# Sliding-window attention and a tanh-shrink MLP: scores of two pairs of heads as one group from batch 3 on

## The chip, the core and the metric

The kernel runs on one core of a Trainium2 chip. A core has TensorE (matmuls), VectorE, ScalarE, GpSimd (POOL in the profile), SyncE, and 16 DMA engines that the queues of SyncE (SP) and GpSimd feed. The metric is device time in microseconds, from the start of the program to its end. Several runs were timed, and one execution was recorded by the profiler; the times of single instructions below are from that one.

## The reference

For 8 batches of 8 heads, with 576 positions and 64 channels a head, each position attends to itself and the 63 before it. The heads of a position are then put side by side (512 channels), and 4608 such tokens go through two layers:

```python
scores = (1 / sqrt(64)) * q @ k.T                 # B=8, H=8, S=576, D=64
mask = (rel >= 0) & (rel < 64)                    # rel = row - column
attn = softmax(where(mask, scores, -1e9))
x = (attn @ v).transpose(0, 2, 1, 3).reshape(4608, 512)
h = x @ w_in                                      # 512 x 2048
out = (h - tanh(h)) @ w_out                       # 2048 x 512, float32 out
```

Inputs and output are float32; the kernel computes its matmuls in bf16.

## The kernel before, in words

**One script sets the order.** Every piece of work is a small step function. `PLAN` (L605) is a long text of words such as `Rp.12.2.4`; `play` (L600) calls the step of that name with these numbers, one after the other. The tile framework runs with a manual schedule, so each engine issues its instructions in the order of the words, and the framework adds the waits that the data need. The letters p, a, v and s at the end of a word name the engine: GpSimd, ScalarE, VectorE, SyncE.

**Attention.** The 8 heads of a batch form 4 pairs; pair `g % 4` of batch `g // 4` has heads `g % 4` and `g % 4 + 4`. The 576 positions are cut in 9 windows of 64 queries, and a window needs 128 keys. Scores are computed with the keys in the 128 rows of the result, so a pair has 9 x 2 products of 128 x 64. There are three forms of it:

- Batch 0 (`BY_HEAD`): one product per head and window, with 64 rows of contraction. A product with `hide` first puts a large negative number where the window ends.
- Batches 1 to 3: `Rp.g.grp.bank` (`scores`, L272) computes three windows at once, with 128 rows of contraction; the q of the two heads stands in `qT` as two blocks with zeros beside them. `Rx` (L310) is the exponential of it. In batch 3 the keys are already in `kw`, put there by DMA transposes.
- Batches 4 to 7: `S.g` (`tile_scores`, L297) has 18 products of 64 x 64 contraction rows and queries, from `kw` and `qw`, which DMA transposes fill. The two heads of a pair lie in the upper and lower half of the rows and write two different PSUM banks, 3 and 4; the ninth window goes to columns 448 to 511 of banks 5 and 7. `Sx.g.0` and `Sx.g.1` are the exponentials (128x1024 and 128x128).

`M.g` (`masking`, L398) multiplies the exponentials by the mask on VectorE. `PP.g` (`pv_pairs`, L418) multiplies two pairs with v, whose tile has a column of ones, into banks 5 to 7 (36 products). `DR` and `DN` (L430, L435) divide by the sums. For batches 0 to 2 `Xp`/`Xc` transpose the result on TensorE and copy it into the chunk tile `xT`; from batch 3 on `Y.b` (`x_dma`, L488) does it with two DMA transposes.

**How q and k come in.** For batches 0 to 2 `lk`/`lq` (`load`, L93) load a pair in rows of 96 partitions; `ck`/`cq` (`cast`) put the heads side by side; `Fp`/`Ep` are six transposes on TensorE (L252), and `Fc`, `Ec`, `Ea`, `Eb` (`put`) copy the result out of PSUM. From batch 3 on `lr.b.i.h` (`load_k`, L157) loads 128 rows of k for half of the heads, cast to bf16 on the way, into a tile laid out pair by pair; `tk.b.i` (`tr_k`, L163) is the DMA transpose on SyncE's queue into `kw`. `qr` and `tq` (L168, L173) do the same for q from batch 4 on. For batch 3, `LQ.3` loads all of q as `lq` does, and it goes on by `cq`, `Ep`, `Ea` and `Eb`. `LV.b.i` loads v, and `Z` copies parts of it to the other half of the partitions.

**The layers.** Tokens are taken in 9 chunks of 512. `H.c.m` (`hp_mm`, L504) is one of 16 tiles of the first layer: four matmuls of 128x512 into bank 0, 1 or 2. `A` is the tanh on ScalarE (L516), `G` the subtraction on VectorE (L522). `W.c.s.part` (`yp_mm`, L537) is a quarter of the second layer for 128 tokens: four matmuls. `O.c.s` copies 128 tokens out of PSUM and sends them to memory on SyncE's queue. `H` of a tile waits until `G` has freed the bank two tiles before.

**Queues.** All loads are issued by GpSimd, in the order of the plan; all transposes and outputs by SyncE, in the order of the plan. A DMA that has to wait for its data holds up all behind it in its queue. `U.n` is n matmuls on a tile of zeros (L219) that keep TensorE busy at the start; `i`, `h`, `n` build the identity, `hide` and the mask on GpSimd, `N` puts the mask into PSUM, and `mt`, `mv`, `mq`, `mk` are memsets on VectorE. `wi` and `wo` load the weights.

Of the kernel before, what the change touches and what calls it, by code (L numbers as in the profile page):

```python
# [7 lines left out]
F32 = mybir.dt.float32  # L8
# [7 lines left out]
def kernel(  # L16
# [41 lines left out]
    mask = ps[:, 6, 480:512].bitcast(BF16)  # L58
# [4 lines left out]
    K_BY_DMA = (3, 4, 5, 6, 7)  # L63
    BY_HEAD = (0,)
    BY_TILE = (4, 5, 6, 7)
    NR, NPT, NROW = 2, 4, 3
    SPLIT = 0
    NKR = 4 if SPLIT else NR
# [5 lines left out]
    PT = [const.tile([128, NJ, 128], BF16, name=f"pt{i}") for i in range(NPT)]  # L74
# [4 lines left out]
    qw = [const.tile([128, NP, S], BF16, name=f"qw{i}") for i in range(2)]  # L79
    rows_all = {n: [const.tile([128, H, E * D], BF16, name=f"{n}all{i}") for i in range(2)] for n in "qk"}  # L80
# [72 lines left out]
    def token_rows(b, n="k"):  # L153
        t = rows_all[n][b % 2].rearrange("p h f -> p (h f)")[:, 0:(NF + 1) * H * D]
        return t.rearrange("p (i r h d) -> p i r h d", r=NP, h=2, d=D)

    def load_k(b, i, h):  # L157

        c = min(128, S - 128 * i)
        nc.gpsimd.dma_start(out=token_rows(b)[0:c, i, :, h, :],  # L160
                            in_=k[b, NP * h:NP * h + NP, 128 * i:128 * i + c].rearrange("r p d -> p r d"))

    def tr_k(b, i):  # L163
        c = min(128, S - 128 * i)
        nc.sync.dma_start(out=kw[b % 2][:, :, 64 + 128 * i:64 + 128 * i + c],
                          in_=token_rows(b)[0:c, i].rearrange("p r h d -> p (r h d)"), transpose=True)

    def load_q(b, i, h):  # L168
        c = min(128, S - 128 * i)
        nc.gpsimd.dma_start(out=token_rows(b, "q")[0:c, i, :, h, :],  # L170
                            in_=q[b, NP * h:NP * h + NP, 128 * i:128 * i + c].rearrange("r p d -> p r d"))

    def tr_q(b, i):  # L173
        c = min(128, S - 128 * i)
        nc.sync.dma_start(out=qw[b % 2][:, :, 128 * i:128 * i + c],
                          in_=token_rows(b, "q")[0:c, i].rearrange("p r h d -> p (r h d)"), transpose=True)
# [32 lines left out]
    def pads_q(i):  # L209
        nc.vector.memset(qT[i], 0.0)  # L210

# [60 lines left out]
    def scores(g, grp, bank):  # L272
        sp, js = group(g, grp, bank)
        first = g not in hidden_by_product
        kt = kT[g % NKR] if g // NP not in K_BY_DMA else kw[g // NP % 2][:, g % NP]
# [18 lines left out]
    def tile_spot(j, h):  # L294
        return ps[:, 3 + h, 64 * j:64 * j + 64] if j < 8 else ps[:, 5 + 2 * h, 448:512]

    def tile_scores(g):  # L297
        b, pr = divmod(g, NP)
        for j in range(NJ):
            for h in range(2):  # L300
                r = slice(64 * h, 64 * h + 64)
                nc.tensor.matmul(tile_spot(j, h), kw[b % 2][r, pr, 64 * j:64 * j + 128],  # L302
                                 qw[b % 2][r, pr, 64 * j:64 * j + 64], start=True, stop=True)
# [10 lines left out]

    halves = {}

    def half_rows(s):
        if not halves:
            t = g_pool.tile([128, M, TOK], BF16, tag="gT", name="early")
            t = t.rearrange("p m t -> p (m t)")  # L320
            n = H * 8 * D
            halves["k", 0], halves["q", 0] = t[0:32, 0:n], t[0:32, n:2 * n]
            n = H * 10 * D
            halves["q", 1], halves["k", 1] = t[32:64, 0:n], t[64:96, 0:n]
        return {n: halves[n, s].rearrange("p (h f) -> p h f", h=H) for n in "qk"}

    def half_span(s):
        return 256 * s, 8 + 2 * s

    def load_half(n, s):  # L330
        t0, e = half_span(s)
        nc.gpsimd.dma_start(out=half_rows(s)[n],
                            in_=(q if n == "q" else k)[0, :, t0:t0 + 32 * e].rearrange("h (p e) d -> p h (e d)", e=e))

    def half_bank(s, bank):
        e = half_span(s)[1]
        return ps[:, bank, :].bitcast(BF16)[:, 0:32 * e].rearrange("c (e p) -> c e p", e=e)

    def half_tr(n, g, s, bank):
        src, tp, r = half_rows(s)[n], half_bank(s, bank), {"k0": 0, "q0": 0, "q1": 32, "k1": 64}[f"{n}{s}"]  # L340
        for e in range(half_span(s)[1]):
            for h in range(2):
                nc.tensor.transpose(tp[64 * h:64 * h + 64, e, :], src[:, g + NP * h, D * e:D * e + D],
                                    ident[r:r + 32, r:r + 32])

    def half_put(n, g, s, bank, eng):
        t0, e = half_span(s)
        to = kT[g][:, 64 + t0:64 + t0 + 32 * e] if n == "k" else qp[g][:, t0:t0 + 32 * e]
        move(eng, to.rearrange("c (p e) -> c p e", e=e), half_bank(s, bank).rearrange("c e p -> c p e"))

    def half_group(s, bank):
        n = 4 + s
# [372 lines left out]
```

## Time and profile before

| | us |
|---|---|
| median of three runs | 313.98 (312.68 to 313.98) |
| span of the profiled execution, first to last instruction | 314.8 |
| TensorE busy | 301.9 |
| VectorE busy | 185.5 |
| ScalarE busy | 159.1 |
| GpSimd busy, issue of its DMAs included | 126.4 |
| H matmuls (L508), 576 of 0.22 us a start | 141.2 busy |
| W matmuls (L551), 530 recorded | 132.0 busy |
| first H step (H.0.0) begins | 25.57 |

In the profile's lists a line like `L302 PE MATMUL ps<-qw,kw ... x288` means: line 302 of the kernel, TensorE, output tile `ps` from `qw` and `kw`, 288 of them. Matmuls are pipelined: the busy time of one (194 ns for a 64-column one) is longer than the distance to the next (about 20), so costs on the path are read from starts. PEclk is the granted clock of TensorE, 1.00 for full speed. A bracket at the end of a line, `[2.31 <-DMA kw<-kall]`, is idle time before the instruction and what ended it. The profiled execution took 0.8 us more than the median of the runs.

### The profile page before, as it was taken

The page shows a single profiled execution, that of the slowest core. Times are in us where ns is not written, and L with a number is a line of the kernel's source. Part 1 is how long each engine was busy: PE and PEld are TensorE (multiplying, and loading weights), DVE is VectorE, ACT ScalarE, POOL GpSimd, SP SyncE. Part 2 cuts the span into 40 slices and gives each one's busy share as a digit, 9 for nine tenths or more (in the row PEclk, how much of TensorE's full clock was granted, in tenths as well). Part 3 has the DMA queues.
Part 4 walks back from the last instruction along what each step waited for, and adds up shares of the span by engine and source line. Part 5 has one row for each costly group of instructions (what it writes and reads, how often), then busy time and mean ns, then how long its engine had stood idle before and what let it go on. Part 6 is the DMA issues. An engine that isn't in the chain of part 4 may idle for free.

```text
span 314.8 us, 6266 instructions
## 1 busy us (share of the span) xinstructions
PE 301.9 (96%) x2480; PEld 159.4 (51%) x2510; DVE 185.5 (59%) x320; ACT 159.1 (51%) x286; POOL 126.4 (40%) x180
## 2 busy tenths in 40 slices
PE   7889899999999969999999999999999999999996
PEld 2565555656655534554455445455444444544443
DVE  3586786499976645784766556767645524533410
ACT  3588963698764524623735364445633433343301
POOL 8991656896992884077800965000000000000000
PEclk9999999999999998999999999999999999999999
DMA  9999999999999999999945999991004010000102
GB/s 158 145 179 204 170 205 185 194 148 115 107 132 138 155 141 141 173 99 158 154 78 116 116 156 155 153 130 50 34 35 108 33 67 35 33 33 35 67 33 101
DMA packets 127789, 36.75 MB, mean 117 GB/s; under 512 B 115600, under 2 KB 122256, under 8 KB 127760
## 3 DMA queue, kind: packets, MB, share of 16 engines
q0 software_dynamic: 88000, 18.07, 73.3%
q1 hardware_dynamic: 39760, 18.29, 29.6%
q8 instruction: 19, 0.31, 0.4%
q14 instruction: 10, 0.08, 0.1%
HBM read 36.70 MB, written 9.44 MB: 147 GB/s over the span
## 4 chain that ended last, share of the span: by engine, by line
PE 82%; DMA 5%; POOL 5%; DVE 3%; issue 2%; ACT 1%; SPq 1%; POOLq 0%; DVEq 0%
PE ps L551 37%; PE ps L508 36%; PE ps L425 3%; DMA wi<-in_moe_w_in_dram 3%; DMA kw<-kall 3%; PE ps L302 2%; PE ps L291 2%; POOL kall L109 1%; DVE gT L522 1%; POOL vw L144 1%; POOL qall L109 1%; PE ps L544 1%; PE ps L252 1%; PE ps L474 1%; DVE qt L91 0%
## 5 line engine op out<-in xcount | busy, mean ns | idle before, releaser
L522 DVE TENSOR_TENSOR gT<-ps,th 128x512 bf16<-128x512 f32 x144 | 97.8, 687 | 78.6 <-ACT th L516 77.4
L508 PE MATMUL ps<-xT,wi 128*128 128x512 bf16 x576 | 141.2, 381 | 0.9 <-DVE gT L522 0.5
L551 PE MATMUL ps<-w_out_sb,gT 128*128 128x512 bf16 x530 | 132.0, 380 | 2.0 <-issue 0.7
L516 ACT ACTIVATE th<-ps 128x512 f32<-128x512 f32 x144 | 84.8, 598 | 96.0 <-PE ps L508 93.6
L508 PEld LDWEIGHTS <-wi 128*128 128x128 bf16 x576 | 63.0, 114 | 55.2 <-issue 1.6
L551 PEld LDWEIGHTS <-gT 128*128 128x128 bf16 x560 | 53.5, 98 | 60.4 <-issue 1.3
L160 POOL DMA_DIRECT2D kall<-in_k_dram x50 | 37.4, 762 | 28.3 <-DMA kw<-kall 23.1
L144 POOL DMA_DIRECT2D vw<-in_v_dram x35 | 31.0, 889 | 19.8 <-PE ps L425 16.4
L170 POOL DMA_DIRECT2D qall<-in_q_dram x40 | 30.1, 777 | 1.4 <-DMA vw<-in_v_dram 1.1
L89 ACT ACTIVATE ysb<-ps 128x512 f32<-128x512 f32 (+2 forms) x23 | 13.3, 580 | 28.3 <-PE ps L551 26.9
L312 ACT ACTIVATE pt<-ps 128x384 bf16<-128x384 f32 (+2 forms) x44 | 22.7, 517 | 8.4 <-PE ps L291 7.3
L400 DVE TENSOR_TENSOR pt<-pt,ps 128x1152 bf16<-128x1152 bf16 x28 | 20.9, 745 | 6.2 <-ACT pt L308 6.1
L308 ACT ACTIVATE pt<-ps 128x128 bf16<-128x128 f32 (+1 forms) x32 | 19.6, 650 | 7.0 <-PE ps L302 6.5
L445 DVE TENSOR_TENSOR xs<-ps,rcp 128x384 bf16<-128x384 f32 x28 | 15.1, 550 | 0.2
L91 DVE COPY ysb<-ps 128x512 f32<-128x512 f32 x14 | 9.6, 684 | 9.1 <-PE ps L551 9.1
L219 PE MATMUL ps<-warm 128*128 128x512 bf16 x27 | 9.4, 493 | 2.2 <-DVE warm L200 2.1
L425 PEld LDWEIGHTS <-pt 128*64 128x64 bf16 x504 | 9.1, 111 | 4.2 <-issue 1.7
L425 PE MATMUL ps<-vw,pt 128*64 128x65 bf16 x504 | 10.7, 197 | 0.0
L89 ACT ACTIVATE qt<-ps 64x576 bf16<-64x576 bf16 x16 | 10.2, 639 | 0.4 <-DVE qt L91 0.3
L433 DVE RECIPROCAL rcp<-ps 128x18 f32<-128x18 f32 x14 | 3.7, 267 | 10.9 <-PE ps L425 10.1
L109 POOL DMA_DIRECT2D qall<-in_q_dram x11 | 7.2, 658 | 6.9 <-DMA wi<-in_moe_w_in_dram 6.9
L302 PEld LDWEIGHTS <-kw 64*128 64x128 bf16 x288 | 5.3, 97 | 8.8 <-issue 6.3
(73 smaller groups left out, 169.8 us busy)
## 6 DMA issues: line engine op xcount, KB each, us to landing
out_dram<-ysb SPq DMA_DIRECT2D x35, 256.0 KB, 2.4
vw<-in_v_dram POOLq DMA_DIRECT2D x28, 128.0 KB, 6.3
kall<-in_k_dram POOLq DMA_DIRECT2D x40, 64.0 KB, 4.9
w_out_sb<-in_moe_w_out_dram POOLq DMA_DIRECT2D x4, 512.0 KB, 8.0
qall<-in_q_dram POOLq DMA_DIRECT2D x32, 64.0 KB, 5.1
kall<-in_k_dram POOLq DMA_DIRECT2D x11, 144.0 KB, 6.1
qall<-in_q_dram POOLq DMA_DIRECT2D x11, 144.0 KB, 5.2
vw<-in_v_dram POOLq DMA_DIRECT2D x16, 64.0 KB, 6.9
```

What stands on the lines that cost most here:

```text
L89: nc.scalar.activation(o, i, ACT.Copy)
L144: nc.gpsimd.dma_start(out=w[:, 2 * i + 1, :, 0:D] if i < NF else w[64:128, 2 * i, :, 0:D], in_=v[b, :, 128 * i:128 * i + n].rearrange("h p ...
L160: nc.gpsimd.dma_start(out=token_rows(b)[0:c, i, :, h, :], in_=k[b, NP * h:NP * h + NP, 128 * i:128 * i + c].rearrange("r p d -> p r d"))
L170: nc.gpsimd.dma_start(out=token_rows(b, "q")[0:c, i, :, h, :], in_=q[b, NP * h:NP * h + NP, 128 * i:128 * i + c].rearrange("r p d -> p r d"))
L308: nc.scalar.activation(PT[g % NPT][:, js, :].rearrange("p i (h t) -> p i h t", h=2), sp, ACT.Exp, scale=scale)
L312: nc.scalar.activation(PT[g % NPT][:, js[0]:js[0] + len(js), :].rearrange("p i (h t) -> p i h t", h=2), sp, ACT.Exp, scale=scale)
L400: nc.vector.tensor_tensor(p, p, mask.unsqueeze(1).to_broadcast([128, 2 * NJ, 64]), ALU.mult)
L425: nc.tensor.matmul(ps[r, bank, 65 * i:65 * i + 65], PT[(g + r2) % NPT][:, j, r], vw[b % 2][:, j, p0 + r2 + NP * h, :], start=True, stop=True)
L508: nc.tensor.matmul(hp, w_in_tile(ki, m), chunk_tile(c)[:, n.start // 64:n.stop // 64, ki % 2, 64 * (ki // 2):64 * (ki // 2) + 64], start=( ...
L516: nc.scalar.activation(th[:, n], hp, ACT.Tanh)
L522: nc.vector.tensor_tensor(gT[c][:, m, columns(s)], hp, th, ALU.subtract)
L551: nc.tensor.matmul(yp, gT[c][:, m, s * 128:(s + 1) * 128], w_out_sb[:, m, :], start=n == 1 and i == 0, stop=n == 4 and i == 3)
```

## The change

From batch 3 on, two pairs of heads are scored as one step `S.g` (g even): 36 products. The loads keep the heads in their natural order, so 128 rows of `kw` hold heads 2m and 2m+1, which belong to two neighbouring pairs. The first pair of the group then lies in rows 0 to 63 and the second in rows 64 to 127, and they write banks 3, 4 and 5, 6. The ninth window of both goes to the first 256 columns of bank 7; there the second pair's two products use all 128 rows, with a new tile `q8`, whose upper half is zeros and whose lower half is filled by a copy `tz.b`. The exponentials are `Sx.g.0` and `Sx.g.1` (1024 columns, one pair each) and `Sx.g.2` (256 columns, both pairs). The mask moves from bank 6 to bank 7, and the four tiles `PT` become parts of one.

Batch 3's q goes by `qr.3` and `tq.3` as the later batches' do: `LQ.3`, its four casts, 24 transposes on TensorE and eight copies out of PSUM are gone. `lr` and `qr` load all eight heads of 128 rows at once, 5 loads for a batch instead of 10. The order of all steps is a new one. Functions that no step of the plan called are removed.

```diff
-    mask = ps[:, 6, 480:512].bitcast(BF16)
+    mask = ps[:, 7, 480:512].bitcast(BF16)
...
-    PT = [const.tile([128, NJ, 128], BF16, name=f"pt{i}") for i in range(NPT)]
+    PT_all = const.tile([128, NPT, NJ, 128], BF16, name="pt")
+    PT = [PT_all[:, i] for i in range(NPT)]
...
+    q8 = [const.tile([128, NP, 64], BF16, name=f"q8{i}") for i in range(2)]
...
-        return t.rearrange("p (i r h d) -> p i r h d", r=NP, h=2, d=D)
-
-    def load_k(b, i, h):
+        return t.rearrange("p (i h d) -> p i h d", h=H, d=D)
+
+    def load_k(b, i, n="k"):
         c = min(128, S - 128 * i)
-        nc.gpsimd.dma_start(out=token_rows(b)[0:c, i, :, h, :],
-                            in_=k[b, NP * h:NP * h + NP, 128 * i:128 * i + c].rearrange("r p d -> p r d"))
+        nc.gpsimd.dma_start(out=token_rows(b, n)[0:c, i],
+                            in_=(q if n == "q" else k)[b, :, 128 * i:128 * i + c].rearrange("h p d -> p h d"))
...
+    def load_q(b, i):
+        load_k(b, i, "q")
...
+    def pads_q8():
+        for i in range(2):
+            nc.vector.memset(q8[i][0:64], 0.0)
...
-    def tile_spot(j, h):
-        return ps[:, 3 + h, 64 * j:64 * j + 64] if j < 8 else ps[:, 5 + 2 * h, 448:512]
+    def tile_spot(r2, h, j):
+        return ps[:, 3 + 2 * r2 + h, 64 * j:64 * j + 64] if j < 8 else ps[:, 7, 128 * r2 + 64 * h:128 * r2 + 64 * h + 64]
+
+    def tail_q(b, eng):
+        move(eng, q8[b % 2][64:128], qw[b % 2][64:128, :, 64 * NJ - 64:64 * NJ])
 
     def tile_scores(g):
-        b, pr = divmod(g, NP)
-        for j in range(NJ):
-            for h in range(2):
-                r = slice(64 * h, 64 * h + 64)
-                nc.tensor.matmul(tile_spot(j, h), kw[b % 2][r, pr, 64 * j:64 * j + 128],
-                                 qw[b % 2][r, pr, 64 * j:64 * j + 64], start=True, stop=True)
+
+        b, n = g // NP, g % NP // 2
+        for h in range(2):
+            nc.tensor.matmul(tile_spot(1, h, 8), kw[b % 2][:, n + 2 * h, 64 * NJ - 64:64 * NJ + 64],
+                             q8[b % 2][:, n + 2 * h, :], start=True, stop=True)
+        for h, j in [(h, j) for h in range(2) for j in range(8)] + [(0, 8), (1, 8)]:
+            for r2 in range(1 if j == 8 else 2):
+                r = slice(64 * r2, 64 * r2 + 64)
+                nc.tensor.matmul(tile_spot(r2, h, j), kw[b % 2][r, n + 2 * h, 64 * j:64 * j + 128],
+                                 qw[b % 2][r, n + 2 * h, 64 * j:64 * j + 64], start=True, stop=True)
 
     def tile_probs(g, part):
-        js = slice(8 * part, 8 + part)
-        sp = ps[:, 5:8:2, 448:512].unsqueeze(1) if part else ps[:, 3:5, :].rearrange("p h (i t) -> p i h t", t=64)
-        nc.scalar.activation(PT[g % NPT][:, js, :].rearrange("p i (h t) -> p i h t", h=2), sp, ACT.Exp, scale=scale)
+        if part == 2:
+            o = PT_all[:, g % NPT:g % NPT + 2, 8, :]
+            sp = ps[:, 7, 0:256].rearrange("p (r t) -> p r t", r=2)
+        else:
+            o = PT[(g + part) % NPT][:, 0:8, :].rearrange("p i (h t) -> p i h t", h=2)
+            sp = ps[:, 3 + 2 * part:5 + 2 * part, :].rearrange("p h (i t) -> p i h t", t=64)
+        nc.scalar.activation(o, sp, ACT.Exp, scale=scale)
...
     PLAN = """
-        mt.0 mv.0 mt.1 lk.3.p lq.0.s lk.1.p u ck.1.a lq.1.p LV.0.1 cq.0.a lk.0.s i mv.1 mk U.13 cq.1.v mq.1 U.1
-        LV.0.3 Ep.1.3 Fp.1.2 Ec.1.3.v lq.3.p ck.0.v U.4 U.1.3 h Fc.1.2.a LV.0.2 Fp.0.2 LV.0.0 LV.0.4 Rp.1.1.4
...
-        qr.5.2.0 G.2.11 A.2.10 H.2.13 M.14 DN.12.1 A.2.13 PP.14 G.2.10 W.1.3.2 DR.14 DN.14.0 DN.14.1 H.2.12
-        tk.4.1 DN.14.2 W.1.3.3 G.2.13 A.2.12 S.17 Sx.17.1 Sx.17.0 H.2.15 G.2.12 H.2.14 Y.3 S.16 tq.5.4 O.1.3.a
...
+        u lk.1.p lk.5.p lk.3.p lq.1.p ck.5.v mt.1 cq.1.v mv.1 U.13 lq.0.s LV.0.2 lq.3.p LV.0.3 lk.2.p i LV.0.1
+        U.4 cq.0.v LV.0.0 lk.0.s mq.0 ck.1.a ck.0.v U.4 Fp.1.2 mq.1 Fc.1.2.v Ep.1.3 mv.0 h U.2 Ec.1.3.a Ep.0.3
+        Rp.1.1.4 Fp.0.2 Rp.1.0.0 Ec.0.3.a Fc.0.2.a Fp.3.2 Rx.1.1.4 Rx.1.0.0 Fc.3.2.v mk mt.0 Z.0 lq.2.p Rp.0.0.0
+        Rx.0.0.0 Ep.3.3 Rp.0.1.4 Ec.3.3.a Rx.0.1.4 Rp.3.0.0 Rx.3.0.0 LV.0.4 P.0 Ep.2.3 lq.5.p Ec.2.3.a D.0
...
+        Xp.2.0.0.3 H.1.15 lr.4.3 DN.10.2 DN.10.0 H.1.14 W.1.0.0 A.1.15 Xc.2.0.0.3.a DN.10.1 Xp.2.1.0.3 A.1.14
+        Xc.2.1.0.3.a tq.3.1 W.1.0.2 Xp.2.1.1.3 G.1.14 G.1.15 Xc.2.1.1.3.a W.1.0.3 H.2.1 H.2.0 W.1.0.1 A.2.1
+        G.2.1 lr.4.1 qr.4.3 tz.3.a LV.3.2 H.2.3 lr.5.4 S.12 A.2.0 A.2.3 tq.4.4 G.2.0 H.2.2 qr.5.2 Sx.12.0
...
+        A.2.9 Sx.14.2 Sx.14.1 Sx.14.0 tq.4.0 W.1.2.3 H.2.8 G.2.9 M.15 A.2.8 M.14 tq.5.2 lr.6.1 tk.4.2 H.2.11
+        W.1.2.2 tk.4.0 tq.4.1 PP.14 G.2.8 DR.14 H.2.10 W.1.2.1 DN.14.2 tz.4.a A.2.11 A.2.10 G.2.11 H.2.13
+        O.1.2.a G.2.10 A.2.13 lr.5.0 qr.5.1 DN.14.1 DN.14.0 G.2.13 H.2.12 Y.3 W.1.3.2 W.1.3.1 H.2.15 A.2.15
+        A.2.12 qr.5.3 LV.4.3 qr.5.4 qr.5.0 S.16 W.1.3.3 G.2.15 G.2.12 W.1.3.0 lr.6.3 qr.6.4 qr.6.2 lr.6.2
```

More of the change, by code (lines that the diff above doesn't have):

```diff
@@ L165, in tr_k @@
         nc.sync.dma_start(out=kw[b % 2][:, :, 64 + 128 * i:64 + 128 * i + c],
[L166 to L171, printed above, removed]
+                          in_=token_rows(b)[0:c, i].rearrange("p h d -> p (h d)"), transpose=True)
+    def load_q(b, i):
+        load_k(b, i, "q")
     def tr_q(b, i):
@@ L175, in tr_q @@
         nc.sync.dma_start(out=qw[b % 2][:, :, 128 * i:128 * i + c],
[L176 removed]
+                          in_=token_rows(b, "q")[0:c, i].rearrange("p h d -> p (h d)"), transpose=True)
     w_in_r = moe_w_in.rearrange("(ko ki) f -> ki ko f", ki=128)
@@ L274, in scores @@
         first = g not in hidden_by_product
-        kt = kT[g % NKR] if g // NP not in K_BY_DMA else kw[g // NP % 2][:, g % NP]
+        kt = kT[g % NKR]
         n = len(js)
@@ L313, in probs @@
                              ACT.Exp, scale=scale)
[L315 to L344, printed above, removed]
```

209 lines of the change are left out of this document (71 added, 138 removed).

## The prediction

> **What bounds the kernel now.** I read the page first, then the same busy times by stage, then the instructions in order of time around the one stage that stands out, then the chain that ended last, then the groups by line. From the page, busy time by engine, and the slices of TensorE and of its clock:
>
> ```profile
> PE 301.9 (96%) x2480; PEld 159.4 (51%) x2510; DVE 185.5 (59%) x320; ACT 159.1 (51%) x286; POOL 126.4 (40%) x180
> PE   7889899999999969999999999999999999999996
> PEclk9999999999999998999999999999999999999999
> ```
>
> TensorE is busy from end to end, so a step off TensorE is worth something only where TensorE waits for it. One slice in the middle has a dent, in busy time and in clock. By stage (after the sum: busy us of PE, PEld, DVE, ACT, POOL, then clock, DMA share, GB/s):
>
> ```profile
> 62.50:88.00 25.50, 25.21 (x255) 15.47 (x254) 23.16 (x42) 21.48 (x43) 21.96 (x30) 1.00 1.64 124
> 112.00:116.50 4.50, 2.19 (x27) 1.08 (x26) 1.01 (x2) 1.33 (x3) 3.39 (x5) 1.00 1.92 168
> 116.50:120.00 3.50, 3.28 (x25) 1.33 (x25) 0.75 (x1) 2.23 (x5) 3.50 (x6) 0.51 2.09 166
> 146.00:312.00 166.00, 164.60 (x1150) 82.72 (x1166) 85.22 (x135) 70.90 (x123) 25.86 (x34) 1.00 0.64 84
> ```
>
> From 146 us on nothing but TensorE matters. At 112 it stands still for over 2 us, and for 3.5 us after that it runs at half clock. What it waits for, in order of time on TensorE:
>
> ```profile
> 112.51 0.23 PE L302 MATMUL ps<-qw,kw 64*128 64x64 bf16 x4
> 115.06 0.38 PE L302 MATMUL ps<-qw,kw 64*128 64x64 bf16 x14 [2.31 <-DMA kw<-kall]
> 115.37 2.52 PE L508 MATMUL ps<-xT,wi 128*128 128x512 bf16 x8
> ```
>
> and on SyncE's queue before it:
>
> ```profile
> 105.36 0.33 SPq L567 DMA_DIRECT2D out_dram<-ysb  x1
> 105.74 3.05 SPq L165 DMA_TRANSPOSE kw<-kall  x2
> ```
>
> The first score step of batch 4 waits for its last key transpose, which SyncE issued behind an output. From the chain (start, length), what a score step of 18 matmuls costs on the path, and the step behind it:
>
> ```profile
> 145.98 0.86 PE ps L508 x4
> 147.21 0.99 PE ps L508 x4
> ```
>
> The first ends at 146.84 and the next begins at 147.21: 0.37 us for S.20 between them, and the step behind it is 0.13 longer than its 0.86.
>
> **The sum** is made against the profiled execution's span of 314.8 us; the median of the runs is 313.98, 0.8 us less.
>
> *Batch 3 leaves the old score form, and two pairs form one step.* Removed: 12 steps Rp of three 128-column matmuls and 4 steps Ep of six transposes. In order of time an Rp begins at 103.51 and the next matmul comes at 103.67: 0.16 each, 1.9 together. An Ep at 31.45 is followed at 31.70: 0.25 each, 1.0. Also removed: 16 steps S at 0.37+0.13, 8.0. Added: 10 steps S of 36 matmuls. 36 of 64 columns are 2 x 0.37; two of them now use all 128 rows and two have no partner in the other row half, so I add 0.02, and 0.13 behind the step: 0.89 each, 8.9. Sum -2.0. Bounds: if the row halves no longer overlap, 36 matmuls at half of an Rp matmul's 53 ns (0.16/3; 64 columns for 128) are 0.96, +2.0 for ten, so 0 altogether; if the 0.13 vanishes, -3.3. The nearest row is the old step itself, which alternates row halves and two banks in the same way.
>
> *Steps put behind the first H:* U.1 (0.22: five took 1.24 at 8.22), Rp.5.2 (0.16) and N (about 0.06) follow it now: +0.4, since TensorE is dense there.
>
> *The wait at batch 4.* 2.3 us idle, and 3.5 us at clock 0.51 cost another 1.7: 4.0. Before, only one W step (0.86) stood in the plan between the last key transpose and S.17. In the new order eight steps, PP.14 and seven H and W, stand between tq.4.1 and S.16: 0.69+7x0.86 = 6.7 us, against medians of 4.2 and 4.6 from issue to landing, and no output stands among the last three transposes. I take all of it: -4.0. Bounds 0 (the wait merely moves) and -4.0. The Trainium skill, "TensorE: Matmul & The Clock Gate", Part 1, has the clock halved after an idle window of about 3.4 us; by that rule a 2.3 us wait would keep full speed, its removal would be worth 2.3 only, and the sum would end 1.7 higher. The trace does not agree: the idle time here was 2.3, and the clock fell all the same.
>
> *Casts and copies of batch 3.* Eight copies qt<-ps (639 ns on ScalarE, 758 on VectorE) and four casts of q (834 and 442) go; and of exponentials, 12 of 487 and the 32 of the old S form (1024 and 276) become three a group: two of 1024 and one of 256 columns, between the 276 of 128 and the 487 of 384. That takes some 8 us off ScalarE and VectorE at 62 to 88 us, where VectorE is busy 23.2 of 25.5 us; but TensorE idles only 0.3 there. I take 0, bounds -1 and +1. The five small copies tz (64 partitions, 256 columns: under the 382 of 128x256) lie on ScalarE and VectorE behind H and W: 0. The mask goes from bank 6 to bank 7, both written by PP, PT becomes one tile of the same four parts, and the removed `half_` functions were called by no step: no instruction more or less, 0.
>
> *Loads.* 90 loads of half the heads (762 and 777 ns on POOL) and LQ.3 (794) become 50 of all heads. The nearest row is the v load of that very shape, 889. POOL: 68.3 down to 44.5 us. No wait of TensorE after H.0.0 is put down to a load, so 0; bounds -1 and 0. Batch 3's q comes in 128 KB pieces (v's landed in 6.3 us) instead of one of 576 KB (9.1): the same bytes, 0, but with a deadline at S.12 now. Its five transposes take 5x1.2 us of SyncE's queue, between outputs: 0 unless S.12 comes first (below).
>
> *The start.* VectorE's second step is now the cast ck.5, whose load is POOL's second, where lk.1 was, which landed at 6.4. Behind it queue cq.1 (its load is fourth instead of third: 7.1+0.65), mv.1, cq.0, mq.0, ck.0, mq.1 and then the copy Fc.1.2, for which the first scores wait. From 7.75: 0.4, mv.1 0.8, cq.0 0.58, mq.0 0.54, ck.0 0.58, mq.1 0.54, copy 0.76: done at about 12, where the first score step began at 9.7. Three more loads of 0.66 stand ahead of LV.0.4, so P.0 moves from 15.4 to some 17.5. Against it: wi.0 is issued 2 us earlier (a v load of 0.81 and the mask's 1.2 go behind it), and the old stage had 2.3 us of ScalarE idle before 16.2. From the first scores on ScalarE is close packed: 14 copies and exponentials of about 0.65 from 12.9 end at 22.0, P.2 and its sums at 24.2, two transposes and their copies at about 26.2, where H.0.0 began at 25.57. +0.7; bounds -0.5 and +2.4 (all of the delay at Fc.1.2).
>
> *H.0.8.* Just before it TensorE idled 0.74 us for the copy Fc.6.3. With the groups' durations, ScalarE's steps between H.0.0 and H.0.8 rise from 7.6 to 8.3 us, beside 7.5 of TensorE: +0.4, bounds -0.7 and +0.8.
>
> *New tight places.* PP.14 and PP.22 follow their S by four H or W steps, 3.45 us. In that time ScalarE must do 1.02+1.02+about 0.4 and VectorE the last mask, 0.75: 3.2, and 0.19 for the last matmul to end, so 3.4 with nothing else in these queues; one tanh (0.6) that comes first costs 0.5. S.14 and S.18 follow PP by 3.45; VectorE has 0.27+3x0.55 and one or two of 0.69, 3.3 at most. +0.6 in all; bounds 0 and +5 (0.5 at each of ten groups).
>
> Sum: -2.0+0.4-4.0+0.7+0.4+0.6 = -3.9, a span of 310.9, a median of 310.1.
>
> **The rivals.** *No new wait at all:* the start's delay hides, the tight places fit, H.0.8 loses its 0.7, and the lighter engines give 1 at 62 to 88. 314.8-2.0+0.4-4.0-0.7-1.0 = 307.5, a median of 306.7. For it: the page shows no loss after 146 us with the same kind of order. Against: ScalarE and VectorE are close packed until 88.
>
> *The wait moves:* somewhere in batches 3 to 7 another transpose comes 2 us late, and 4.0 comes back: 314.9, a median of 314.1, within 0.5%. For it: Y.3 (5.6 us to landing) has eleven steps, 9 us, from PP.14 to H.3.1, of which VectorE's sums take 2.5; that leaves 1 us to spare.
>
> *Slower, by one place: S.12.* All its operands now come through SyncE, by ten transposes. The last loads of k for batch 3 were issued at 66.5 to 68 before, and two v and two q loads now stand ahead of them. If the queue gets going only at 67, the last one lands at 67+10x1.3+4.4 = 84.4. S.12's own place: H.2.1 began at 86.84 before; five Rp, two Ep and a W (2.2) are gone from ahead of it, 1.1 are added, and four steps (3.45) come up to S.12: about 89. It decides against the change once the last transpose lands after 92.8: 3.8 us of waiting and 1.7 of half clock undo the 3.9 and give 1.6 more. Then 316.4 and up. For it: POOL was 22.0 of 25.5 us busy there. Against: half as many issues.
>
> *Slower by the PSUM turn:* a group holds five banks, so its exponentials, masks, PP, sums and the next S are one chain. At 1 us for each of ten groups it gives 310.9-0.6+10 = 320.3, a median of 319.5; it decides from 0.6 us a group on.
>
> **How the numbers follow.** A change of 0.5% (1.6 us) is about what this kernel's runs can tell. My forecast (308.5 to 312.4) has 0.45, no new wait 0.20, the moved wait 0.14, S.12 0.11, the PSUM turn 0.10. So faster 0.65, same 0.14, slower 0.21; the likeliest's own range is 308.5 to 312.4. The range reaches from 306.5, just under the second case, to 316.5, where S.12 begins to cost: outside lie 0.05 below and 0.14 above.
>
> **What would show it.** Right: TensorE idle for no more than 0.5 us at a score step, clock 1.00 from 30 us on, 36 matmuls of S in 0.75 to 0.80 us of the path, H.0.0 at 26 to 26.5, POOL near 103 us busy. Wrong: a wait of the score line for a transpose at batch 3, a wait of PP for the masks or of S for VectorE's sums of over 0.5 us in most groups, or H.0.0 after 27.5.

## The result, and the profile after

The kernel after takes 328.53 us in the median (325.58 to 332.49, four runs) beside 313.56 for the kernel before on the same chip. The ratio is 1.046 (95% interval 1.041 to 1.052): slower by some 14.5 us, where 310.1 and "faster" were forecast. The profiled execution of after took 327.7 us, its span is 326.0: 11.2 more than the span of 314.8 that the sum started from. Runs over 1.5% above the fastest of their kernel are left out of all ratios here; the profiled executions of e4, e8, e12 and e13 were such runs, so of these only landings, first steps and, for e13, the waits in one table are read.

Of the page, busy time by engine, and the slices of TensorE and its clock:

```profile
PE 304.3 (93%) x2489; PEld 161.6 (50%) x2522; DVE 184.4 (57%) x318; ACT 155.5 (48%) x269; POOL 103.5 (32%) x139
PE   8599999999999949999759999999999999999996
PEclk9859999999999987999979999999999999999999
```

GpSimd is lighter by 23 us, as forecast. The dent in the middle has become three, and there is a new one at the start. By stage (columns as in the prediction; the last but one adds up the times of the DMA packets over 16 engines and can pass 1):

```profile
62.50:88.00 25.50, 25.37 (x244) 15.06 (x243) 22.32 (x41) 18.47 (x37) 15.71 (x19) 1.00 2.19 151
112.00:146.00 34.00, 28.95 (x251) 14.58 (x255) 16.59 (x28) 12.69 (x21) 9.87 (x13) 0.90 1.41 137
146.00:180.00 34.00, 28.17 (x227) 14.33 (x230) 17.98 (x30) 13.80 (x24) 11.63 (x14) 0.95 1.48 132
200.00:323.00 123.00, 122.00 (x798) 61.89 (x809) 60.04 (x96) 49.24 (x83) 0.00 (x0) 1.00 0.19 58
```

From 112 to 180 us TensorE is idle for 10.9 us of 68; from 200 on, for 1.0 of 123. In order of time on TensorE, the places where it stands still:

```profile
116.08 1.03 PE L437 MATMUL ps<-xT,wi 128*128 128x512 bf16 x4
121.79 1.86 PE L437 MATMUL ps<-xT,wi 128*128 128x512 bf16 x4 [4.68 <-DMA xT<-xs]
123.45 1.91 PE L480 MATMUL ps<-w_out_sb,gT 128*128 128x512 bf16 x4
...
157.55 1.05 PE L437 MATMUL ps<-xT,wi 128*128 128x512 bf16 x4 [1.66 <-DMA xT<-xs]
...
167.50 1.21 PE L354 MATMUL ps<-vw,pt 128*64 128x65 bf16 x36 [3.72 <-DVE vw L150]
```

The first wait is chunk 3's first layer for `Y.3`, the DMA transpose of batch 3's result; steps of four behind it take 1.9 instead of 1.03, at half clock:

```profile
121.70:125.20 3.50, 3.41 (x9) 1.22 (x9) 0.69 (x1) 0.60 (x1) 0.00 (x0) 0.50 1.55 198
```

By the starts of the steps the loss is 6.9 in all. The second wait is chunk 4's for `Y.4` (1.9). The third is `PP.20`, for `Z.5` on VectorE, which waits for the v load `LV.5.0` (5.2 with the slow steps behind it). Together 13.9 us (6.89, 1.85 and 5.16), all of them for a DMA. The chain that ended last names the same two kinds, and shows a score group (rows that begin at 90 us):

```profile
90.37 0.86 PE ps L437 x4
91.29 0.63 PE ps L310 x34
91.92 1.85 PE ps L437 x8
...
110.86 10.89 DMA xT<-xs
...
151.62 10.73 DMA vw<-in_v_dram
```

`Y.3` takes 10.89 us from issue to landing, where it took 5.73 before (here and below, a landing of `Y` is that of the first of its two transposes, for which the next chunk waits). The chain's row for v ends where VectorE's idle time begins; by the load's own record LV.5.0 landed at 165.87, 14.3 us after its issue, and `Z.5` began at 165.95. Before, LV.5.0 was issued at 118.2 and landed after 8.4. The group of 36 begins at 91.23, where the first-layer step ends, and the next step begins at 91.92: 0.69, and the two steps behind it are 0.13 longer than 2 x 0.86. So 0.82 a group where 0.89 was forecast.

Queue rows and the DMA slices of the page, after:

```profile
DMA  9999999999999999999994999313004101000012
q1 hardware_dynamic: 42224, 18.88, 31.2%
```

and before:

```profile
DMA  9999999999999999999945999991004010000102
q1 hardware_dynamic: 39760, 18.29, 29.6%
```

In both, the DMA engines are over 90% busy for the first half of the span; batch 3's q transposes add 0.59 MB to that. The records of the loads issued between 60 and 180 us give this:

| loads of k, q, v rows | before | after |
|---|---|---|
| most open at once | 8 | 8 |
| mean KB open when one is issued, itself counted | 404 | 733 |
| mean us from issue to landing | 5.2 | 9.2 |

Eight are open at most in both, and k's and q's are twice as big.

The start, as one stage, before:

```profile
9.00:25.50 16.50, 14.44 (x291) 9.53 (x288) 11.29 (x23) 11.90 (x23) 14.24 (x23) 1.00 1.32 166
```

and after:

```profile
9.00:25.50 16.50, 13.15 (x210) 7.95 (x211) 9.66 (x22) 8.88 (x15) 13.52 (x21) 0.69 1.16 128
```

H.0.0 begins at 30.2 us instead of 25.6, P.0 at 20.1 instead of 15.4, and TensorE runs at 0.69 of its clock there. So the 11.2 are: start +4.6, three new waits +13.9, the wait at batch 4 gone -4.0, the score form -2.7, and -0.6 for the rest.

### The profile page after: what moved, and what is told of

It is laid out like the page before. It is cut to its first block, busy times and chain, and to the rows that moved or that the text cites. A ratio compares the mean times of both kernels' runs of the same rounds, so it can differ in the third digit from the quotient of the medians.

```text
span 326.0 us, 6251 instructions
## 1 busy us (share of the span) xinstructions
PE 304.3 (93%) x2489; PEld 161.6 (50%) x2522; DVE 184.4 (57%) x318; ACT 155.5 (48%) x269; POOL 103.5 (32%) x139
## 4 chain that ended last, share of the span: by engine, by line
PE 75%; DMA 9%; issue 6%; DVE 4%; POOL 4%; ACT 1%; SPq 0%; DVEq 0%; POOLq 0%; ACTq 0%
PE ps L480 32%; PE ps L437 32%; DMA vw<-in_v_dram 4%; DMA xT<-xs 3%; PE ps L354 3%; PE ps L253 1%; POOL vw L143 1%; DVE gT L451 1%; PE ps L310 1%; PE ps L473 1%; POOL qall L159 1%; DMA qw<-qall 1%; POOL kall L108 1%; PE ps L292 1%; PE ps L249 1%
## 5 line engine op out<-in xcount | busy, mean ns | idle before, releaser
L143 POOL DMA_DIRECT2D vw<-in_v_dram x35 | 30.3, 872 | 31.2 <-PE ps L354 23.6
L159 POOL DMA_DIRECT2D kall<-in_k_dram x25 | 21.4, 860 | 32.3 <-DMA kw<-kall 27.9
L320 ACT ACTIVATE pt<-ps 128x1024 bf16<-128x1024 f32 (+1 forms) x30 | 22.8, 811 | 3.8 <-PE ps L310 3.6
L159 POOL DMA_DIRECT2D qall<-in_q_dram x25 | 21.6, 873 | 7.9 <-DMA qw<-qall 5.2
L324 ACT ACTIVATE pt<-ps 128x384 bf16<-128x384 f32 (+2 forms) x32 | 16.7, 529 | 9.1 <-PE ps L292 6.5
L90 DVE COPY ysb<-ps 128x512 f32<-128x512 f32 x15 | 10.3, 687 | 8.4 <-PE ps L480 8.3
L108 POOL DMA_DIRECT2D kall<-in_k_dram x11 | 7.3, 665 | 4.7 <-DMA wi<-in_moe_w_in_dram 3.9
L90 DVE COPY qt<-ps 64x576 bf16<-64x576 bf16 x9 | 6.8, 756 | 2.9 <-PE ps L292 1.3
L292 PEld LDWEIGHTS <-kt 128*128 128x128 bf16 x72 | 5.7, 98 | 4.5 <-issue 0.4
L292 PE MATMUL ps<-qt,kt 128*128 128x128 bf16 x72 | 8.0, 219 | 0.0
```

The costliest lines, as they stand in the source:

```text
L90: eng.tensor_copy(o, i)
L143: nc.gpsimd.dma_start(out=w[:, 2 * i + 1, :, 0:D] if i < NF else w[64:128, 2 * i, :, 0:D], in_=v[b, :, 128 * i:128 * i + n].rearrange("h p ...
L159: nc.gpsimd.dma_start(out=token_rows(b, n)[0:c, i], in_=(q if n == "q" else k)[b, :, 128 * i:128 * i + c].rearrange("h p d -> p h d"))
L292: nc.tensor.matmul(sp[:, i], kt[:, 64 * j:64 * j + 128], qT[g % NR][:, :, 64 * j:64 * j + 64], start=first, stop=first or i == n - 1)
L320: nc.scalar.activation(o, sp, ACT.Exp, scale=scale)
L324: nc.scalar.activation(PT[g % NPT][:, js[0]:js[0] + len(js), :].rearrange("p i (h t) -> p i h t", h=2), sp, ACT.Exp, scale=scale)
```

## The experiments

A theory and two rivals stood at the outset. **D:** the late landings come from what is in flight ahead of a transfer, since as many loads are open as before and each is twice as big. **O:** they come from the place in the queues alone. **Start:** the late start is the new order of VectorE's fills and casts. Ratios are to the kernel before on the same chip, with 95% intervals; after itself has 1.046. Of an edit to the plan only the words that move are shown, with a few of their neighbours.

### Half loads: e1_half_loads

```diff
-        nc.gpsimd.dma_start(out=token_rows(b, n)[0:c, i],
-                            in_=(q if n == "q" else k)[b, :, 128 * i:128 * i + c].rearrange("h p d -> p h d"))
+        for h in range(2):
+            r = slice(NP * h, NP * h + NP)
+            nc.gpsimd.dma_start(out=token_rows(b, n)[0:c, i, r],
+                                in_=(q if n == "q" else k)[b, r, 128 * i:128 * i + c].rearrange("h p d -> p h d"))
```

> The kernel after, with each load of all eight heads' k or q rows cut into two of four heads (64 KB instead of 128), in the same places of the order; nothing else. Theory D (depth): the waits of H.3.0 and H.4.0 come from transposes that stand behind twice the bytes in flight, since as many loads are open at once as before and each is twice as big. Then Y.3 lands some 6 us after its issue instead of 10.9 and Y.4 6 instead of 9.9, the idle time ahead of H.3.0 falls from 4.7 to under 1 and that of H.4.0 from 1.7 to under 0.5, and the time falls by 6 to 9 us to some 320. Theory O (order): the transposes are late by their place in SyncE's queue and the size of a load doesn't matter; then both waits stay within 1 us and the time stays at 326 to 329, or rises because 50 more issues of 0.77 us go back onto POOL, which by either theory reads about 120 us busy instead of 103.5.

Measured: 1.034 (1.026 to 1.042). Y.3 lands after 6.6 us and Y.4 after 6.4; idle time ahead of the first steps of chunks 3 and 4 (H.3.1, which the expectations call H.3.0, and H.4.0) is 0.7 together instead of 6.3. So theory D's landings came out, but the time fell by 4 us only: a v load that came later in GpSimd's queue (LV.3.2) held `Z.3` on VectorE, which cost 2 us at H.2.7, and PP.20's wait grew to 5.1.

### v first: e2_v_first

```diff
-        ... LV.6.3 qr.6.0 ... LV.6.2 LV.5.1 LV.5.3 ... LV.5.2 qr.7.0 LV.5.0
+        ... LV.5.1 LV.5.3 LV.5.2 LV.5.0 lr.7.2 ... LV.6.3 qr.6.0 ... LV.6.2 ... qr.7.0
```

> The kernel after, with the four v loads LV.5.1, LV.5.3, LV.5.2 and LV.5.0 moved in the order ahead of lr.7.2; nothing else. Theory P: PP.20 waits because these loads stand behind a load of batch 6's v (LV.6.3, which waits for PP.18) and behind lr.7.2 in POOL's queue. Then the 3.7 us wait ahead of PP.20 and its half clock go, 4.5 to 5 us, to some 322 to 323; Y.3's wait stays, at 4 us or a little more. Theory D (the loads land late wherever they are issued, since too much is in flight): PP.20 keeps most of its wait and the time stays within 1.5 us of 327.7.

Measured: 1.018 (1.010 to 1.025), 9 us off. LV.5.0 is issued at 122.5 instead of 151.6 and PP.20's loss is 0.5. It had stood behind LV.6.3, for which GpSimd waited 6.05 us (for PP.18 to free v's tile), and behind lr.7.2, for which it waited 10.5. So a better place in the queue is enough to remove that wait. It doesn't show that depth had no part in it: LV.5.0 lands after 13.3 us here too, and with the 8.4 of before it would have landed in after at about 160, in time for PP.20 (an estimate: 151.6 + 8.4). Y.4's wait went too (it lands after 6.1), Y.3's fell to 2.8.

### The old start: e3_old_start

```diff
-        u lk.1.p lk.5.p lk.3.p lq.1.p ck.5.v mt.1 cq.1.v mv.1 U.13 ...
+        mt.0 mv.0 mt.1 lk.3.p lq.0.s lk.1.p u ck.1.a lq.1.p LV.0.1 cq.0.a lk.0.s i mv.1 mk U.13 cq.1.v mq.1 U.1 ...
```

> The steps up to the first step of the first layer (H.0.0) in the order of the kernel before, and behind them all the other steps in the order of the kernel after; loads and scores of the kernel after. If the late start is the price of the new order alone: H.0.0 at 25.6 instead of 30.2, clock back to full speed before 25 us, and the time falls by 4 to 5 us to some 323. If the four rows put off behind H.0.0 or the waits of the later batches eat it: under 2 us of gain.

Measured: 1.041 (1.034 to 1.048). H.0.0 begins at 26.0 and the clock of the stage is 1.00 again, so the start's delay is the order's. But 1.6 us came off, which the intervals don't tell from nothing, not 4: H.0.7 now waited 2.6 us for VectorE, which stood at the cast cq.6 for a load that landed at 35.5. What the start gained was given back 10 us later.

### Loads of batch 6 later: e4_hold_loads

```diff
-        ... S.16 W.1.3.3 G.2.15 G.2.12 W.1.3.0 lr.6.3 qr.6.4 qr.6.2 lr.6.2 O.1.3.v H.2.14 ... H.3.1
+        ... S.16 W.1.3.3 G.2.15 G.2.12 W.1.3.0 O.1.3.v H.2.14 ... H.3.1 lr.6.3 qr.6.4 qr.6.2 lr.6.2
```

> The kernel after, with the four loads lr.6.3, qr.6.4, qr.6.2 and lr.6.2 (128 KB each, for batch 6) moved from just behind Y.3 to just behind H.3.1; nothing else. Theory D: they are open when Y.3's transposes are under way and delay them; then Y.3 lands 6 to 8 us after its issue instead of 10.9, the wait of H.3.0 falls from 4.7 to under 2, and 3 to 7 us come off, less what the later loads cost PP.20 (0 to 2). Theory O: Y.3's landing and the wait stay within 1 us, and the time is the same or longer.

Measured: 325.4 to 334.2 us. The edit did nothing of what it meant: the four loads were issued at 113.3 to 116.1, as before. GpSimd's queue follows only its own waits, not TensorE's place in the plan. To hold a load back, something in its own queue must wait.

### Whole loads in the kernel before: e5_before_whole

```diff
-    def load_k(b, i, h):
+    def load_k(b, i):
-        nc.gpsimd.dma_start(out=token_rows(b)[0:c, i, :, h, :],
-                            in_=k[b, NP * h:NP * h + NP, 128 * i:128 * i + c].rearrange("r p d -> p r d"))
+        nc.gpsimd.dma_start(out=token_rows(b)[0:c, i].rearrange("p r h d -> p (r h) d"),
+                            in_=k[b, :, 128 * i:128 * i + c].rearrange("h p d -> p h d"))
```

> The kernel before, with the two loads of half the heads (64 KB) of each k and q row tile of batches 3 to 7 made one load of all heads (128 KB) at the place of the first of the two; the score form, the start and every other place stay. Changed in the computation: the rows lie in natural order of heads, so a score pair of batches 3 to 7 holds two neighbouring heads while v's pairing stays; the time of each step is that of its shapes. Theory D: bigger loads at the same number open are enough for late transposes; Y.3 lands 9 to 11 us after its issue instead of 5.7 and TensorE waits 3 to 6 us at H.3.0 or at a score step of batches 4 and 5; 316 to 321. Rival, the new order makes the waits (theory O): with POOL relieved of some 25 us the loads come earlier, the wait at S.17 stays or shrinks, 310 to 314.

Measured: 1.006 (1.004 to 1.008), 2 us, between the two expectations. Y.3 lands after 8.2 us instead of 5.5 to 5.7, and TensorE waits for it:

```profile
121.81 1.89 PE L508 MATMUL ps<-xT,wi 128*128 128x512 bf16 x8 [0.85 <-DMA xT<-xs]
```

So larger loads alone make the landing later, but the old order left enough room: 0.85 us of wait. Size alone is not the loss. (This execution also waited 1.8 us for a weight load at H.0.0, ahead of all that the edit changes.)

### Fills first: e8_fills_first

```diff
-        u lk.1.p lk.5.p lk.3.p lq.1.p ck.5.v mt.1 cq.1.v mv.1 ...
+        u lk.1.p lk.5.p lk.3.p lq.1.p mt.1 mv.1 mq.0 mq.1 mv.0 mt.0 ck.5.v cq.1.v ...
```

> The kernel after, with the fills mt.1, mv.1, mq.0, mq.1, mv.0 and mt.0 in front of VectorE's first cast ck.5, where VectorE is idle from 1 to 7 us; nothing else. If the late start is VectorE's queue (fills among the casts that the first scores wait for, and LV.0.4 and Rp.0.0.0 behind mv.0 and mt.0): the first score step at 11 instead of 11.8 to 12.4, P.0 at about 17.5 instead of 19 to 20, H.0.0 1.5 to 3 us earlier, and the time 1.5 to 3 lower. If it is the order of the loads or of the casts: H.0.0 moves by under 1 us.

Measured: 1.033 (1.024 to 1.042). By their first weight loads P.0 begins at 17.6 and H.0.0 at 27.0, against 18.7 to 20.1 and 28.2 to 30.2 in five executions with after's start (after, e1, e2, e4, e10). This one execution would make VectorE's fills 1 to 3 us of the late start. But the old start itself gave H.0.0 at 25.2 to 27.5 in thirteen executions, so the share is an indication, and the rest was not taken apart.

### Mended order, whole and half: e6_mended, e7_mended_half

Both have e2's and e3's edits, and these; the second has e1's halves as well.

```diff
-        ... wi.0 wi.1 wi.2 lv.1.1.0 lq.6.p ... Ep.7.3 cq.6.v Rx.4.1.4 G.0.5 G.0.4 ... lr.5.2 ... LV.3.2
+        ... wi.0 wi.1 lq.6.p wi.2 lv.1.1.0 ... Ep.7.3 Rx.4.1.4 G.0.5 G.0.4 cq.6.v ... LV.3.2 ... lr.5.2
```

> The kernel after with four edits of order, loads left at 128 KB: the start of the kernel before (as in the run on the old start, with the cast cq.6 behind G.0.4 and its load lq.6 ahead of wi.2, so that H.0.7 doesn't wait behind it), the four v loads of batch 5 ahead of lr.7.2, and LV.3.2 in the place of lr.5.2. If the losses add up (start 3.5 to 4.6, PP.20 5, H.0.7 2.2 not come back) and Y.3's wait alone stays: 314 to 317 by the clock of the runs, about as before. By theory D Y.3 still waits 2.5 to 5 us.

> The order of the mended kernel, and each k or q load of all heads cut into two of four heads (64 KB). Theory D: Y.3's wait goes too, 4 to 6 us less than the mended kernel: 308 to 312, faster than before. Theory O, or if POOL's 40 more issues make v and k late instead: no better than the mended kernel.

Measured: 1.016 (1.013 to 1.020) and 1.011 (1.008 to 1.015). In the first Y.3 lands after 11.3 us and the wait is 5.1, as theory D had it. In the second Y.3 still takes 8.9 and the wait is 2.5, and TensorE waits 2.3 us more at S.16 (1.25 and 1.08), where transposes of batch 4 come late: halving the loads is no cure in this order, though it was in after's.

### The kernel before, once more: e9_before_again

> The kernel before, unchanged, profiled once more. If the wait at batch 4 (2.3 us idle at the first score step of batch 4 and 3.5 us at half clock, 4.0 together) belongs to every execution, it is here too and the mean clock reads 0.994 again. If it belonged to that one execution, TensorE waits under 0.5 us at that step, the clock is 1.00 and the span some 311, 3 to 4 us less than the 314.8 on which the sum was made.

Measured: span 312.4, clock 1.000. In order of time at the same place:

```profile
113.04 0.23 PE L302 MATMUL ps<-qw,kw 64*128 64x64 bf16 x4
114.19 0.38 PE L302 MATMUL ps<-qw,kw 64*128 64x64 bf16 x14 [0.92 <-DMA kw<-kall]
114.50 1.92 PE L508 MATMUL ps<-xT,wi 128*128 128x512 bf16 x8
```

The wait is 0.92 and no half clock follows. Of 85 runs of the kernel before made beside these experiments, four show a clock of 0.995 (spans of 313.1 to 314.1); the others lie at 0.999 or more, with spans of 310.2 to 312.8. By that a wait that costs half clock, as the 2.3 with its 1.7 did, belongs to a few executions.

### Holding loads back: e10_hold_y3, e11_mended_hold, e12_mended_hold2

```diff
+    held = const.tile([128, D], BF16, name="held")
+    def hold(b):
+        nc.gpsimd.tensor_copy(held, xs[b % 2][:, 0, 2, :])
...
-        ... tq.5.2 lr.6.1 tk.4.2 ... lr.5.0 qr.5.1 DN.14.1 DN.14.0 G.2.13 H.2.12 Y.3 ... qr.5.3 LV.4.3
+        ... tq.5.2 LV.4.3 tk.4.2 ... DN.14.1 DN.14.0 gx.3 lr.6.1 lr.5.0 qr.5.1 G.2.13 H.2.12 Y.3 ... qr.5.3
```

`gx.3` is `hold(3)`. e10 has it in after's plan, e11 in the mended plan; e12 adds `gx.4` ahead of LV.6.3, qr.6.0, LV.6.2 and qr.7.3.

> The kernel after, with the loads that stand ahead of Y.3 in the DMA engines held back until Y.3 can be issued: a small copy on POOL that reads the last normalized rows of batch 3 stands ahead of lr.6.1, lr.5.0 and qr.5.1 in POOL's queue, so these and all later loads come some 3 us later, and LV.4.3 (needed for batch 4's sums) is moved ahead of it. Sizes, bytes and all other places stay. If what is in flight ahead of a transpose sets when it lands: Y.3 lands 5 to 7 us after its issue instead of 10.9, the wait of H.3.0 falls from 4.7 to under 1.5, and 5 to 7 us come off (321 to 323). If the size of the loads that run beside it, or the place in SyncE's queue, sets it: Y.3 lands after 9 to 11 us as before and nothing is gained.

> The mended order (old start, v of batch 5 and LV.3.2 earlier) with the same holding back ahead of Y.3. If in-flight bytes set Y.3's landing: its wait of 5.1 us and the half clock behind it go, 5 to 7 us less than the mended kernel's 318.1, so 311 to 313, no slower than the kernel before. Otherwise 317 to 319.

> As the kernel before it, and a second copy of that kind that holds LV.6.3, qr.6.0, LV.6.2, qr.7.3 and what follows back until batch 4's rows are normalized, for Y.4. By the in-flight reading Y.4 lands in 5 to 7 us instead of 8.7 and its 0.4 to 0.8 us go: 310 to 312.5. Rival: batch 6's loads, 3 us later, make v or the transposes of batches 6 and 7 late; then 312 to 315.

e10 measured: 1.029 (1.026 to 1.032), 5.4 us off, with loads of the same size and number. No load is open when Y.3 is issued, and it lands after 4.8 us. The place where 4.68 us were lost, in order of time:

```profile
114.87 0.70 PE L314 MATMUL ps<-qw,kw 64*128 64x64 bf16 x34
115.73 1.68 PE L484 MATMUL ps<-w_out_sb,gT 128*128 128x512 bf16 x7 [0.16 <-issue]
117.24 1.89 PE L441 MATMUL ps<-xT,wi 128*128 128x512 bf16 x8
```

This is the clearest test: the loads that are open ahead of a transpose set when it lands. The place in SyncE's own queue (theory O) doesn't: three transfers of that queue are open when Y.3 is issued in after, and three in e15 below, where no load is open and Y.3 lands after 5.0. Of the 6.9 us of Y.3's wait 5.4 were gained; e10's profiled execution has a wait of 1.7 us for VectorE at H.2.7 that after's doesn't have, as e1's had.

e11: 1.012 (1.009 to 1.015). Y.3 lands after 5.0 and its wait is gone, but S.20 waited 1.9 us for a q transpose of batch 5 whose load had been held. e12: 1.008 (1.005 to 1.012); Y.4 lands after 6.4, but in its profiled execution two held loads came ahead of Y.3, which took 10.2. Neither reached what was expected.

### More transposes alone: e14_more_transposes

```diff
-                          in_=token_rows(b, "q")[0:c, i].rearrange("p r h d -> p (r h d)"), transpose=True)
+                          in_=token_rows(b, "q" if b > 3 else "k")[0:c, i].rearrange("p r h d -> p (r h d)"), transpose=True)
...
-        ... tk.3.2 ... tk.3.3 ... tk.3.4 ...
+        ... tk.3.2 tq.3.2 ... tk.3.3 tq.3.3 ... tk.3.4 tq.3.4 ...
```

> The kernel before, with five more DMA transposes, one behind each of batch 3's key transposes on SyncE's queue: they read the key rows again and write the q tile that batch 5 uses later, so nothing of the result depends on them. This is the DMA traffic that the change adds for batch 3's q, without the new score form and without a deadline. If 0.59 MB more on DMA engines that are busy 9 tenths of the time is a main part of the loss: 2 to 5 us longer, with later landings of batch 4's transposes and Y.3. If not: within 1 us of the kernel before.

Measured: 1.004 (1.002 to 1.006), 1.2 us. Y.3 lands after 5.9. The added traffic costs little by itself, and doesn't make Y.3 late.

### One wait after the other: e13_hold_half, e15_hold_q5, e16_tq5_first, e17_hold_all

e15 is e11 with lr.6.1 behind batch 5's q loads, e13 the same with half loads. e16 changes SyncE's queue in e15, e17 adds two holds to e16 (a third number, as in `gx.4.2`, says which part of the rows the copy reads):

```diff
-        ... S.18 Sx.18.0 tk.6.3 ... W.2.2.3 tk.6.2 M.19 ... tq.5.3 ... S.20 Y.4
+        ... S.18 Sx.18.0 ... W.2.2.3 M.19 ... tq.5.3 ... S.20 Y.4 tk.6.3 tk.6.2
...
-        ... lr.6.4 qr.7.1 PP.18 qr.6.3 ... LV.6.3 qr.6.0 ... LV.6.2 ... qr.7.3 ... DN.18.0
+        ... lr.6.4 PP.18 ... DN.18.0 gx.4.2 qr.7.1 qr.6.3 LV.6.3 qr.6.0 LV.6.2 qr.7.3
...
-        ... DN.22.1 DN.22.0 G.4.8 DN.22.2 ... LV.7.3
+        ... DN.22.1 DN.22.0 G.4.8 DN.22.2 gx.5.3 ... LV.7.3
```

> The mended order with Y.3's forerunners held back, batch 6's first k load put behind batch 5's q loads (since S.20 waited 1.9 us for a transpose of batch 5's q in the held kernel), and the k and q loads in halves of 64 KB. If bytes in flight and order are what is left to mend: no wait over 1 us behind batch 3, 309 to 312, faster than the kernel before. If 64 KB loads make POOL late instead: 314 and up.

> The same order with the loads left at 128 KB. If the order alone was the fault: 311 to 313. If the size also matters for what lands behind them: 2 to 4 us more than with halves, 314 to 316.

> The held order with batch 5's q first, and two key transposes of batch 6 (tk.6.3, tk.6.2) put behind Y.4 on SyncE's queue, so that tq.5.3, the last transpose that S.20 needs, is issued some 4 us earlier. If S.20's 2.7 us wait (3.2 with the half clock) was the last large loss of the change behind H.0.0: the wait falls to under 0.5, the profiled span to 307 to 309, and the time to 309.5 to 312.5, faster than the kernel before. If it moves to Y.4 or PP.20 instead: 313 to 315, as it was.

> As the kernel with tq.5.3 first, and two more holding copies on POOL: one for batch 4's rows ahead of qr.7.1, qr.6.3 and LV.6.3, one for batch 5's rows ahead of LV.7.3, so that Y.4 (10.4 us to landing) and Y.5 (9.8) find few loads ahead of them. If the loads ahead of a transpose are the whole of these waits: Y.4 and Y.5 land in 5 to 7 us, their 4.4 us of waits and half clock fall under 1, and the time is 309.5 to 312, faster than the kernel before by some 0.5%. If each wait only moves on to the next transpose or to v: 313 to 315, not faster.

| kernel | ratio (interval) | Y.3, Y.4, Y.5, us to landing | waits of over 1.2 us behind H.0.0 |
|---|---|---|---|
| e13 | 1.015 (1.011 to 1.019) | 8.4, 8.4, 9.4 | Y.3 3.3, a q transpose 1.5 |
| e15 | 1.005 (1.002 to 1.009) | 5.0, 9.0, 8.0 | S.20 2.7 |
| e16 | 1.001 (0.998 to 1.004) | 5.1, 10.4, 9.8 | Y.4 2.1, Y.5 1.5 |
| e17 | 0.996 (0.993 to 0.998) | 5.2, 6.9, 4.4 | none |

e13 missed: with halves Y.3 was late again and the kernel slower than with whole loads. In its profiled execution the copy let the loads go at 107.1 us, but SyncE came to Y.3 only at 110.3, and four loads of 64 KB stood ahead of it; so e13 doesn't tell what halves do when the holding works. e15 and e16 fell short because each time the next transfer in line was late. In e17 all three transposes land within 6.9 us, and it is the only one that beats both kernels: 311.4 us beside 312.8. Its stages, to set against those of after:

```profile
112.00:146.00 34.00, 33.61 (x282) 17.51 (x286) 21.27 (x35) 16.50 (x28) 18.22 (x22) 1.00 1.89 151
146.00:180.00 34.00, 32.95 (x281) 17.27 (x283) 22.00 (x35) 17.61 (x30) 11.82 (x15) 1.00 1.57 152
```

Here 66.6 of 68 us are busy, with scores, loads and bytes of after. From H.0.0 to the end of the last matmul it takes 280.4 us, the kernel before in e9 283.3: 2.9 less, of which 0.9 is e9's wait at batch 4; the other 2.0 are about what the score form was worth in the sum.

## Why the prediction was wrong, step by step

- **Base.** Two errors. The sum started from a span of 314.8 that holds a 4.0 us wait which most runs don't have in full: e9's span is 312.4, with 0.92 of wait. And a run's time is 1.7 us above its span (327.7 and 326.0 for after), where the prediction (and the table ahead of it) took the median for 0.8 below; a span of 310.9 would have been 312.6 us. With 1.0 for the wait in place of 4.0 the same sum comes to -0.9, within 0.5%.
- **Score form, -2.0:** right in mechanism, measured -2.7 (0.82 a group, not 0.89). The 36 matmuls take 0.69 on the path beside 2 x 0.37, so the row halves still overlap and the bound 0 is excluded.
- **Wait at batch 4, -4.0:** S.16 has no wait, so it is gone as the step said. What it was worth in most runs is about 1.
- **Loads, "0; bounds -1 and 0":** the step that failed. It priced a load by its issue on GpSimd (right: POOL 103.5 us) and excluded a loss because no wait had been put down to a load. But the loads' landing time rose from 5.2 to 9.2, and what else goes through the DMA engines rose with it: three waits, 13.9 us. e10 shows it for Y.3 (no load ahead, 4.8 us, wait gone). At PP.20 (5.2) two things met: the prediction did not walk through the new order of v's loads in GpSimd's queue, where LV.5.0 was issued 33 us later than before, and e2 shows that its place alone can remove the wait; and the load landed after 14.3 us instead of 8.4.
- **"The wait moves":** the rival named the right place, Y.3, and gave it 1 us to spare, from a landing of 5.6 in the trace before. It landed after 10.9. The place was right, the landing time was carried over from a queue that the change itself refilled.
- **Start, +0.7, bounds -0.5 and +2.4:** +4.6 in this execution, and 2.6 to 4.6 over the old start's 25.6 in five. The first scores began near where the forecast had them (12.4 and about 12), but P.0 came at 20.1, not 17.5. LV.0.4 waited 1.9 us in GpSimd's queue for the fill mv.0, moved back on VectorE, and Rp.0.0.0 0.3 for mt.0: the fills were counted for the first scores only, not for these two. The first scores waited 0.73 for `hide` on GpSimd besides. e3 takes away all of the delay, e8 some 1 to 3 us of it in one execution.
- **H.0.8, +0.4:** no loss over 0.35 there. **Tight places, +0.6:** 0.3 at PP.12, nothing else over that. The PSUM turn and S.12, the two rivals on the slow side, did not come; the slow side came by a third way.

The traces bear on one rule. The Trainium skill, "DMA: Bandwidth & Descriptors", section on queues, rings and completion order, has each DMA engine take turns between its queues, a packet at a time; by that one would expect a transpose on SyncE's queue to pass many of GpSimd's loads. The runs don't agree as far as landing goes: 4.4 to 5.2 us with no load ahead (e10, e11, e15, e16, e17), 10.9 with five of 128 KB. In 55 of 57 cases (Y.3, Y.4 and Y.5 in nineteen profiled executions) the transpose lands behind every load issued before it, to within 0.11 us, and ahead of every load issued once its own issue had ended; the other two, Y.4 in e11 and e15, pass two or three loads by up to 4.6 us. The same section of the Trainium skill has a transfer's completion counted only after all earlier writes of that engine, across its queues, which would fit; no run here separates it from a plain queue.

By that order a late landing is the time that the loads issued ahead need to clear.

**What stays open:** that time is no simple function of their bytes. Y.3 of the kernel before lands after 5.7 us with some 416 KB of loads open, that of e1 after 6.6 with 512 KB, that of after after 10.9 with 640 KB, and that of e13 after 8.4 with 256 KB. Nor was the rest of the start taken apart.

## What to carry to other kernels

Where the DMA engines are busy, price a load by what it does to the landing of others, not only by its issue: a load twice as big with as many open nearly doubles what stands ahead of every transpose (404 and 733 KB here). An order written out by hand is one queue per engine, so walk each queue by itself, and hold a load back with something that its own queue must wait for. Before a stall is priced, see in the spans and clocks of other runs whether it is there every time.

## What was not expected of the hardware

- **Half clock does not follow the length of an idle gap.** Windows of e15 and of e16, a gap and what follows it (the column before the last two is the clock):

```profile
138.00:140.90 2.90, 0.23 (x12) 0.13 (x9) 0.69 (x1) 0.52 (x1) 0.00 (x0) 1.00 2.07 163
140.90:144.50 3.60, 3.56 (x37) 1.92 (x37) 0.56 (x1) 0.60 (x1) 2.74 (x4) 1.00 1.53 181
```

```profile
145.00:147.10 2.10, 0.01 (x1) 0.00 (x0) 0.68 (x2) 1.89 (x3) 0.00 (x0) 1.00 1.68 60
147.10:150.60 3.50, 3.45 (x11) 1.46 (x12) 1.26 (x2) 0.60 (x1) 1.76 (x2) 0.67 1.84 154
```

  After 2.71 us of standing still the clock stays at 1.00, after 2.15 it falls to 0.67. (In after it was 0.50 behind 4.68 us.) The prediction weighed a rule of the Trainium skill on this ("TensorE: Matmul & The Clock Gate", Part 1: half clock after an idle window of about 3.4 us, counted in windows that run freely). By it neither gap should have cost clock; the 2.15 did, as the 2.31 of the prediction's profile did, and the measurement decides. Price such a stall with and without its half clock.
- **The second select of the tile `hide` on GpSimd** took 1.99 us in after, 0.29 before; in e1, e2 and e4, which have the same start, the first of the two took 0.96 to 1.51. VectorE was copying and filling beside it; whether that is the cause was not tested.
